# Twelve early loads of an attention and two-MoE kernel issued as 120 and 8 partitions, and one unit's softmax steps in another order

## The chip, the cores and the metric

The kernel runs on 1 core of one Trainium2 chip. The metric is device time in microseconds of one execution. Engines are named as in the profile: PE (TensorE matmul), PEld (its weight loads), DVE (VectorE), ACT (ScalarE), POOL (GpSimd) and SP (SyncE, which here only issues DMAs). A core has 16 DMA engines.

## What is computed

Three stages in a row, each on the output of the one before. Batch 4, 8 heads, 576 positions, head size 64:

```python
scores = scale * np.matmul(q, k.transpose(0, 1, 3, 2))
masks = np.stack([mask_local if h < H // 2 else mask_strided for h in range(H)], axis=0)
attn = softmax(np.where(masks[None], scores, -1e9)); x = attn @ v   # then to (2304, 512)
x = (sigmoid(x @ w_gate) * (x @ w_val)) @ w_out                      # 512 -> 1536 -> 512
x = softplus(x @ w_in) @ w_out2                                      # 512 -> 2048 -> 512
```

The first four heads see a local window of 32 positions, the other four every 32nd position.

## The kernel before, in words

Attention works on 16 units; a unit is one batch and one pair of heads, units 0 and 1 of each batch local, 2 and 3 strided. For a unit, `load` issues its q and K from SP (K of units 0 and 1 from ACT; K of units 2, 3 and 4 as two halves of 64 partitions into `acc` tiles), and `load_v` issues its V. Then, as separate steps: `bias` (a mask product on PE, L1063 or L1075), `scores` (PE, L1095 for units 2 to 4 and L1106 for the others; then DVE's maximum L1124 and subtraction L1125), `exponent` (ACT, L1132), `normalize` (DVE's sum L1139 and reciprocal L1142, POOL's product L1145), `p_transposes` (PE, L1168, then a copy on ACT), `values` (PE, L1188) and `outputs` (ACT L1213, DVE L1216: the high and low halves of x).

The weights come as 64-bit words in pieces of 128 x 512 (`raw`, 512 KB, three buffers, `load_next`, L110). `decode_steps` turns a piece into a high and a low half: first step L132 and L136 on DVE; second step L142 and L149 on DVE, L160 on ACT, L162 and L163 on POOL, and, if it refills, the next `load_next`. A decoding writes two work tiles, f and e; those of the `decp` pool have one buffer each.

The program order of each engine is the order in which the code is written (`manual_schedule`). `first()` is the start of the kernel: units 0 to 4, and the first decodings. `stage(u)` then does one unit each for u from 5 (`START`) on, in four parts with a `yield` after each, and between the parts matmuls of the first MoE (lines L73 to L75, helper `mm3`) are put in. From about 70 us on PE has only MoE matmuls and what little attention is left.

Three more things set when a load starts. `load(..., held=True)`, `load_v(..., held=True)` and `load_next(held=True)` put a one-element memset on POOL (`hold`, L101) that the DMA waits for. The q tiles have three buffers, so q of unit 3 waits until PE is through with the scores of unit 0. And the DMAs take eight completion semaphores in turn: a DMA waits until the one eight before it has landed.

Of the kernel before, what the change touches and what calls it, by code (L numbers as in the profile page):

```python
# [22 lines left out]
P = 128  # L23
# [26 lines left out]
def tile_sparse_attention_moe_moe2(  # L50
# [51 lines left out]

    def load_next(held=False):
        if todo:
            g, m, c = piece = todo.pop(0)
            src = w1[g, m] if g < NG1 else w2[g - NG1, m // 2]
            raw = rawp.tile([P, PIECE], U64, tag="raw", name="raw")
            if held:
                hold(raw.bitcast(F32))
            nc.sync.dma_start(out=raw, in_=src[:, c * PIECE:(c + 1) * PIECE])  # L110
            raws[piece] = raw
            queue.append(piece)
# [764 lines left out]
    def attention():  # L877
        with ExitStack() as actx:
# [48 lines left out]
            def load(i, held=False):  # L927
                b, hp = units[i]
                loc, w, m, ns = dims(i)
                qn, kn = (S, S + STRIDE) if loc else (QPAD, QPAD - HP + SQ)  # L930
                qq = qp.tile([P, QPAD], F32, tag="q", name="qt")
                if held:
                    hold(qq)
                nc.sync.dma_start(out=qq[:, 0:qn], in_=q[b, hp][:, 0:qn])
                if i in paired:
                    kk = paired[i]
                    for h in range(2):
                        rows = slice(h * HP, (h + 1) * HP)
                        nc.sync.dma_start(out=kk[rows, h, 0:kn], in_=k[b, hp][rows, 0:kn])
                else:  # L940
                    kk = kp.tile([P, QPAD], F32, tag="k", name="kt")
                    (nc.scalar if i < 2 else nc.sync).dma_start(
                        out=kk[:, 0:kn], in_=k[b, hp][:, 0:kn]
                    )
                qt[i], kt[i] = qq, kk

            def load_v(i, held=False):
# [8 lines left out]
                n = NL[0] if loc else NS  # L956
                nc.sync.dma_start(out=t[:, 0:n], in_=vl[b, hp] if loc else vs[b, hp - NLP])
                vt[i] = t
# [286 lines left out]
            def first():  # L1245

                decs = [decode_steps(pools, refill) for refill in (False, False, True)]
                swap = lambda: pools.update(f=[other])
# [6 lines left out]
                normalize(0)  # L1255
                load_next(held=True)
                load_v(2)
# [3 lines left out]
                normalize(1)  # L1261
                load_next(held=True)
                load_v(3)
# [8 lines left out]
                normalize(3)  # L1272
                load_next(held=True)
                values(0)
# [17 lines left out]
                pools["scratch"] = None  # L1292
                load_next(held=True)
                load(6)
# [11 lines left out]
                load_next()  # L1306
                next(decs[2])
                yield
                next(decs[2])
                yield  # L1310

            def stage(u):
# [6 lines left out]
                def more():  # L1319
                    if dec:  # L1320
                        next(dec.pop(0))

                if u < NU:
                    bias(u)
                    scores(u)
                if u == START:
                    yield
                if u == START + 2:
# [28 lines left out]
                if u < NU - 2:  # L1357
                    load(u + 2)
                more()
                if u == START + 1:  # L1360
                    exponent(u)
                    nc.scalar.preload_act_table_set("sigmoid_and_others")
                yield
                if u < NU and u != START + 1:
                    exponent(u)
                if len(dec) > 1:
                    more()
                yield
                if u < NU:
                    normalize(u)  # L1370
                values(u - 1)
                outputs(u - 1)
# [211 lines left out]
```

## Times and the profile before

| what | us |
|---|---|
| median of 3 runs | 877.82 |
| the runs | 877.8, 877.82, 880.9 |
| the profiled execution, its own time | 880.17 |
| its span in the trace | 878.0 |

The profiled execution is 2.35 us over the median; 2.17 us of its time lie outside the span. PE is busy 862.9 us of the span; the rows that follow further down are read from this execution. In a row of the timeline the first number is the start in us from the span's start, the second its length, and the bracket at the end is the idle time of the engine just before it, with what ended it.

### The profile page before, as it was taken

What the parts mean: (1) busy time and instruction counts of PE and PEld (TensorE: products, weight loads), DVE (VectorE), ACT (ScalarE), POOL (GpSimd) and SP (SyncE); (2) the same over time, 40 slices, a digit from 0 to 9 for tenths busy, and PEclk for the clock granted to TensorE, in tenths of its full rate; (3) what the DMA queues carried; (4) which work ended last, traced back from release to release, by engine and by line L of the source; (5) the groups of instructions that cost most, each with busy time, mean ns of one, the idle gap of its engine ahead of it and who ended that gap; (6) DMA issues with size and microseconds to landing.
All of it is one profiled execution on the core that took longest, in us unless ns stands there. A gap on an engine that the chain in (4) does not pass through costs nothing.

```text
span 878.0 us, 15217 instructions
## 1 busy us (share of the span) xinstructions
PE 862.9 (98%) x5925; PEld 723.3 (82%) x5925; DVE 600.1 (68%) x897; ACT 422.4 (48%) x684; POOL 490.6 (56%) x394
## 2 busy tenths in 40 slices
PE   7999999999999999999999999999999999999998
PEld 6678788888888888888888888888888888888886
DVE  7887755378888878788865646565757674656574
ACT  4366534233333232333233456666768566655641
POOL 6572511057887788687778525556446963343620
PEclk9899999999999999999999999999999999999999
DMA  9773430044766566557553436655675665545403
GB/s 282 266 249 128 150 130 1 1 144 166 252 230 213 193 241 218 191 196 252 200 185 127 128 101 196 193 195 193 195 259 172 200 213 187 181 141 184 144 1 120
DMA packets 61431, 154.03 MB, mean 175 GB/s; under 512 B 6064, under 2 KB 6576, under 8 KB 61360
## 3 DMA queue, kind: packets, MB, share of 16 engines
q1 hardware_dynamic: 61072, 152.44, 52.1%
q8 instruction: 47, 0.77, 0.4%
q10 hardware_dynamic: 288, 0.62, 0.2%
q14 instruction: 24, 0.20, 0.1%
HBM read 114.76 MB, written 38.27 MB: 174 GB/s over the span
## 4 chain that ended last, share of the span: by engine, by line
PE 72%; DVE 3%; ACT 1%; POOL 1%; issue 1%; DMA 0%; DVEq 0%; POOLq 0%; ACTq 0%; SPq 0%
PE ps_y L73 10%; PE ps_y L74 10%; PE ps_y L75 10%; PE ps_v L74 4%; PE ps_v L75 4%; PE ps_v L73 4%; PE ps_h L74 4%; PE ps_h L75 4%; PE ps_h L73 4%; PE ps_g L74 4%; PE ps_g L75 4%; PE ps_g L73 4%; PE ps_b L73 2%; PE ps_b L74 2%; PE ps_b L75 2%
## 5 line engine op out<-in xcount | busy, mean ns | idle before, releaser
L339 POOL TENSOR_TENSOR b<-b,b 128x512 f32<-128x512 f32 (+1 forms) x42 | 72.4, 1737 | 91.7 <-DVE gl L339 46.2
L313 DVE TENSOR_TENSOR acc<-ps_y,acc 128x512 f32<-128x512 f32 (+1 forms) x100 | 62.1, 633 | 48.0 <-PE ps_y L75 47.6
L252 ACT ACTIVATE gh<-ps_v 128x512 fp32r<-128x512 f32 (+1 forms) x60 | 33.3, 555 | 123.4 <-DVE ps_v L293 123.2
L342 ACT ACTIVATE gh<-b 128x1024 fp32r<-128x1024 f32 (+1 forms) x63 | 57.8, 917 | 40.6 <-DVE b L722 22.7
L478 DVE TENSOR_TENSOR acc<-ps_y,acc 128x512 f32<-128x512 f32 x66 | 44.8, 686 | 39.5 <-PE ps_y L75 38.5
L339 POOL TENSOR_TENSOR gl<-b,gh 128x1024 fp32r<-128x1024 f32 x20 | 49.1, 2456 | 36.5 <-ACT gh L342 36.5
L253 DVE TENSOR_TENSOR gl<-ps_v,gh 128x512 fp32r<-128x512 f32 (+1 forms) x60 | 38.3, 638 | 37.5 <-ACT gh L252 37.5
L199 POOL TENSOR_TENSOR a<-f,e 128x512 f32<-128x512 f32 x32 | 41.4, 1294 | 39.1 <-DVE e L149 39.1
L187 POOL TENSOR_TENSOR pair<-a,pair 128x512 fp32r<-128x512 f32 x32 | 41.5, 1297 | 33.2 <-ACT pair L186 33.2
L339 DVE TENSOR_TENSOR gl<-b,gh 128x1024 fp32r<-128x1024 f32 (+1 forms) x43 | 48.8, 1137 | 14.4 <-ACT gh L342 14.3
L75 PE MATMUL ps_y<-gh,w02l 128*128 128x512 f32 (+1 forms) x144 | 53.7, 373 | 0.4 <-POOL w02l L163 0.4
L73 PE MATMUL ps_y<-gh,w12h 128*128 128x512 f32 (+1 forms) x144 | 54.0, 375 | 0.1
L74 PE MATMUL ps_y<-gl,w12h 128*128 128x512 f32 (+1 forms) x144 | 53.6, 372 | 0.0
L186 ACT ACTIVATE pair<-s 128x512 fp32r<-128x512 f32 x32 | 20.2, 632 | 69.4 <-POOL s L213 54.1
L136 DVE SCALAR_TENSOR_TENSOR f<-raw,ps_x 128x512 uint32<-128x512 uint32 x67 | 46.1, 688 | 9.9 <-POOL w11l L163 2.1
L293 DVE TENSOR_TENSOR ps_v<-ps_v,sg 128x512 f32<-128x512 f32 (+1 forms) x60 | 38.5, 641 | 20.4 <-PE ps_v L75 19.2
L75 PE MATMUL ps_y<-gh,w12l 128*128 128x512 f32 (+1 forms) x140 | 52.2, 373 | 0.2 <-POOL w12l L163 0.2
L73 PE MATMUL ps_y<-gh,w02h 128*128 128x512 f32 (+1 forms) x136 | 51.3, 377 | 0.7 <-ACT acc L311 0.5
L74 PE MATMUL ps_y<-gl,w02h 128*128 128x512 f32 (+1 forms) x136 | 50.7, 372 | 0.2 <-DVE gl L253 0.2
L149 DVE SCALAR_TENSOR_TENSOR e<-raw,ps_x 128x512 f32<-128x512 uint32 x67 | 46.0, 687 | 2.4
L142 DVE TENSOR_SCALAR ps_x<-f 128x512 uint32<-128x512 uint32 x67 | 46.1, 688 | 1.0
L132 DVE TENSOR_SCALAR ps_x<-raw 128x512 uint32<-128x512 uint32 x68 | 46.5, 684 | 0.0
(365 smaller groups left out, 2803.4 us busy)
## 6 DMA issues: line engine op xcount, KB each, us to landing
raw<-in_w_dram SPq DMA_DIRECT2D x68, 512.0 KB, 4.5
in_s<-pair SPq DMA_DIRECT2D x32, 512.0 KB, 3.2
out_s<-pair SPq DMA_DIRECT2D x32, 512.0 KB, 2.9
xh<-in_s SPq DMA_DIRECT2D x64, 256.0 KB, 3.0
xl<-in_s SPq DMA_DIRECT2D x56, 256.0 KB, 3.6
vt<-in_vl_dram SPq DMA_DIRECT2D x8, 640.0 KB, 6.3
out_dram<-acc SPq DMA_DIRECT2D x16, 256.0 KB, 2.2
w10h<-out_s SPq DMA_DIRECT2D x6, 512.0 KB, 4.0
```

Of the source, the lines that this page charges most:

```text
L73: nc.tensor.matmul(ps, lhsT=lh, rhs=rh, start=first, stop=False, **kw)
L74: nc.tensor.matmul(ps, lhsT=lh, rhs=rl, start=False, stop=False, **kw)
L75: nc.tensor.matmul(ps, lhsT=ll, rhs=rh, start=False, stop=last, **kw)
L132: nc.vector.tensor_scalar(out=part, in0=high, scalar1=3, scalar2=0x3FFFFFFF, op0=ALU.logical_shift_left, op1=ALU.bitwise_and,)
L136: nc.vector.scalar_tensor_tensor(out=f, in0=high, scalar=0xC0000000, in1=part, op0=ALU.bitwise_and, op1=ALU.bitwise_or,)
L142: nc.vector.tensor_scalar(out=e, in0=f, scalar1=0xFF800000, scalar2=None, op0=ALU.bitwise_and)
L149: nc.vector.scalar_tensor_tensor(out=e.bitcast(F32), in0=low, scalar=2.0 ** -52, in1=x.bitcast(F32), op0=ALU.mult, op1=ALU.mult,)
L187: nc.gpsimd.tensor_tensor(out=l, in0=src, in1=h.bitcast(F32), op=ALU.subtract)
L313: nc.vector.tensor_tensor(out=y, in0=ps[:, 0:n], in1=y, op=ALU.add)
L339: eng.tensor_tensor(out=out, in0=a, in1=b, op=ALU.subtract)
L342: nc.scalar.activation(out=op[0], in_=src, func=AF.Copy)
L478: nc.vector.tensor_tensor(out=y, in0=ps, in1=y, op=ALU.add)
```

## The change

- `copy_rows` issues a load either as one DMA or as two, of partitions 0 to 119 and 120 to 127. Two are issued for q of units 2, 3 and 4, for V of units 0 to 4, and for the four pieces that `first()` loads with `load_next(held=True)`: twelve loads.
- In `load(3)` the two halves of K are issued ahead of q.
- The third decoding leaves `first()` and is done in `stage(5)`, both its steps in one go, after the scores and the exponent of unit 5. That exponent moves ahead of it, to just after the scores. The decoding that `stage(5)` had of its own starts after `normalize(5)`.

```diff
+    few = 15 * (P // 16)
+
+    def copy_rows(out, src, apart):
+        for rows in (slice(0, few), slice(few, P)) if apart else (slice(0, P),):
+            nc.sync.dma_start(out=out[rows], in_=src[rows])
+
-    def load_next(held=False):
+    def load_next(held=False, apart=False):
...
-            nc.sync.dma_start(out=raw, in_=src[:, c * PIECE:(c + 1) * PIECE])
+            copy_rows(raw, src[:, c * PIECE:(c + 1) * PIECE], apart)
...
-                nc.sync.dma_start(out=qq[:, 0:qn], in_=q[b, hp][:, 0:qn])
+
+                def load_q():
+                    copy_rows(qq[:, 0:qn], q[b, hp][:, 0:qn], NLP <= i <= NPAIR)
+
+                if i != NPAIR - 1:
+                    load_q()
                 if i in paired:
...
+                    if i == NPAIR - 1:
+                        load_q()
...
-                nc.sync.dma_start(out=t[:, 0:n], in_=vl[b, hp] if loc else vs[b, hp - NLP])
+                copy_rows(t[:, 0:n], vl[b, hp] if loc else vs[b, hp - NLP], i <= NPAIR)
...
-                decs = [decode_steps(pools, refill) for refill in (False, False, True)]
+                decs = early_decs
+                decs += [decode_steps(pools, refill) for refill in (False, False, True)]
...
-                load_next(held=True)
+                load_next(held=True, apart=True)
...
                 load_next()
-                next(decs[2])
                 yield
-                next(decs[2])
                 yield
+
+            early_decs = []
...
                 if u == START:
+                    exponent(u)
                     yield
...
-                more()
+                if u > START:
+                    more()
+                else:
+                    next(early_decs[2])
+                    next(early_decs[2])
...
-                if u < NU and u != START + 1:
+                if u < NU and u > START + 1:
                     exponent(u)
-                if len(dec) > 1:
+                if u > START and len(dec) > 1:
                     more()
                 yield
                 if u < NU:
                     normalize(u)
+                if u == START:
+                    more()
```

The line `load_next(held=True)` changes so in four places. What the change moves on the engines stands in the built order. On SP, from the third q load on, before (`qt` is q, `vt` V, `acc2` and `acc0` the homes of K of units 2 and 3; DMAHW0 to 7 are the eight completion semaphores):

```order
L934 DMA qt_148<-in_q_dram 128x622
L939 DMA acc2_65<-in_k_dram 64x612 x2
L934 DMA qt_152<-in_q_dram 128x622 [waits DMAHW1_49,PE_49]
L939 DMA acc0_63<-in_k_dram 64x612 [waits DMAHW0_49]
L939 DMA acc0_63<-in_k_dram 64x612
L957 DMA vt_156<-in_vl_dram 128x1280 [waits DMAHW2_49]
L957 DMA vt_158<-in_vl_dram 128x1280 [waits DMAHW3_49]
L110 DMA raw_331<-in_w1_dram 128x512 [waits DMAHW4_49,Pool_49]
```

and in the changed kernel:

```order
L107 DMA qt_148<-in_q_dram 120x622
L107 DMA qt_148<-in_q_dram 8x622
L950 DMA acc2_65<-in_k_dram 64x612 x2
L950 DMA acc0_63<-in_k_dram 64x612 [waits DMAHW0_49]
L950 DMA acc0_63<-in_k_dram 64x612 [waits DMAHW1_49]
L107 DMA qt_153<-in_q_dram 120x622 [waits DMAHW2_49,PE_49]
L107 DMA qt_153<-in_q_dram 8x622 [waits DMAHW3_49]
L107 DMA vt_158<-in_vl_dram 120x1280 [waits DMAHW4_49]
L107 DMA vt_158<-in_vl_dram 8x1280 [waits DMAHW5_49]
L107 DMA vt_161<-in_vl_dram 120x1280 [waits DMAHW6_49]
L107 DMA vt_161<-in_vl_dram 8x1280 [waits DMAHW7_49]
L107 DMA raw_335<-in_w1_dram 120x512 [waits DMAHW0_49,Pool_49]
```

K of unit 3 no longer stands behind q of unit 3 and its wait for PE, and each split load takes two of the eight semaphores.

On DVE at units 4 and 5 (`sl0` is the softmax tile of unit 4, `sl1` that of unit 5; `raw_411` the third piece, `raw_579` the fourth), before:

```order
L1142 RECIPROCAL st_642<-st_642 128x2x5
L132 TENSOR_SCALAR ps_x_658<-raw_411 128x512
L136 SCALAR_TENSOR_TENSOR f_656<-raw_411,ps_x_658 128x512
L142 TENSOR_SCALAR ps_x_667<-f_656 128x512
L149 SCALAR_TENSOR_TENSOR e_657<-raw_411,ps_x_667 128x512
L1124 TENSOR_REDUCE st_720<-ps_s_677 128x5x2
L1125 TENSOR_TENSOR sl1_110<-ps_s_677,st_720 128x5x2x64
L132 TENSOR_SCALAR ps_x_746<-raw_579 128x512
L136 SCALAR_TENSOR_TENSOR f_744<-raw_579,ps_x_746 128x512
L1139 TENSOR_REDUCE st_720<-sl1_110 128x2x5
```

and in the changed kernel, where the third piece is `raw_420` and the fourth `raw_590`:

```order
L1155 RECIPROCAL st_654<-st_654 128x2x5
L1137 TENSOR_REDUCE st_719<-ps_s_676 128x5x2
L1138 TENSOR_TENSOR sl1_110<-ps_s_676,st_719 128x5x2x64
L138 TENSOR_SCALAR ps_x_746<-raw_420 128x512
L142 SCALAR_TENSOR_TENSOR f_744<-raw_420,ps_x_746 128x512
L148 TENSOR_SCALAR ps_x_750<-f_744 128x512
L155 SCALAR_TENSOR_TENSOR e_745<-raw_420,ps_x_750 128x512
L1152 TENSOR_REDUCE st_719<-sl1_110 128x2x5
L1154 TENSOR_SCALAR st_719<-st_719 128x2x5
L1155 RECIPROCAL st_719<-st_719 128x2x5
L138 TENSOR_SCALAR ps_x_767<-raw_590 128x512
```

The maximum and subtraction of unit 5 now stand ahead of the third decoding, and its sum and reciprocal ahead of the fourth. On ACT the exponent of unit 5 (`sl1`) stood behind a decoding step and a copy, before:

```order
L1132 ACTIVATE sl0_109<-sl0_109 128x640
L160 ACTIVATE w01h_68<-f_656 128x512
L1174 ACTIVATE pt_729<-ps_p_730 128x2x320
L1132 ACTIVATE sl1_110<-sl1_110 128x640
L1213 ACTIVATE xh_61<-ps_o_758 128x320
```

and in the changed kernel it stands ahead of both, and the decoding step has gone behind the copy:

```order
L1145 ACTIVATE sl0_109<-sl0_109 128x640
L1145 ACTIVATE sl1_110<-sl1_110 128x640
L1187 ACTIVATE pt_729<-ps_p_730 128x2x320
L166 ACTIVATE w01h_68<-f_744 128x512
L1226 ACTIVATE xh_61<-ps_o_770 128x320
```

The order of PE's and of POOL's instructions is the same in both kernels.

## Rows read from the trace of the kernel before

**Rows 1.** The page, part 1: busy time, share, instructions.
```profile
PE 862.9 (98%) x5925; PEld 723.3 (82%) x5925; DVE 600.1 (68%) x897; ACT 422.4 (48%) x684; POOL 490.6 (56%) x394
```

**Rows 2.** Waits of PE, 0 to 70 us: total us, times, longest.
```profile
PE ps_s L1095 <- DMA acc<-in_k_dram: 2.3, 2, 1.7
...
PE ps_o L1188 <- issue: 1.1, 2, 1.0
```

**Rows 3.** Timeline, 5.9 to 18 us: SP, DVE, POOL and PE, units 2 and 3.
```profile
5.98 0.33 SPq L934 DMA_DIRECT2D qt<-in_q_dram  x1
...
6.36 1.10 SPq L939 DMA_DIRECT2D acc<-in_k_dram  x2
...
12.69 1.33 PE L1095 MATMUL ps_s<-acc,qt 128*64 128x108 f32 x24 [1.68 <-DMA acc<-in_k_dram]
...
13.02 0.21 DVE L1142 RECIPROCAL st<-st 128x10 f32<-128x10 f32 x1
...
14.07 0.83 DVE L1124 TENSOR_REDUCE st<-ps_s 128x12 f32<-128x648 f32 x1 [0.83 <-PE ps_s L1095]
...
16.92 1.42 POOL L1145 TENSOR_TENSOR ss<-ss,st 128x324 f32<-128x324 f32 x2 [2.11 <-DVE st L1142]
...
17.93 1.02 PE L1168 MATMUL ps_p<-one,ss 128*128 128x128 f32 x6 [0.42 <-ACT acc L1172]
```

**Rows 4.** DMA issues, 6.3 to 6.8 us: count, KB each, us to landing.
```profile
qt<-in_q_dram SPq DMA_DIRECT2D x1, 311.0 KB, 4.1
acc<-in_k_dram SPq DMA_DIRECT2D x1, 153.0 KB, 5.6
```

**Rows 5.** DMA queue of the instructions, 8 to 20 us: packets, MB, share.
```profile
q8 instruction: 2, 0.03, 1.2%
```

**Rows 6.** Stretches: length, busy us by engine, PEclk, DMA share, GB/s.
```profile
8.80:10.00 1.20, 1.05 (x23) 1.09 (x24) 1.20 (x2) 0.65 (x1) 0.00 (x0) 1.00 1.03 230
12.40:14.00 1.60, 1.31 (x25) 1.20 (x25) 0.77 (x3) 0.43 (x1) 0.62 (x1) 1.00 0.98 353
```

**Rows 7.** Timeline, values of unit 1 on PE, 18.9 to 21.4 us.
```profile
18.88 0.55 PE L1188 MATMUL ps_o<-acc,vt 64*64 64x32 f32 x24
...
20.38 1.00 PE L1188 MATMUL ps_o<-acc,vt 64*64 64x32 f32 x48 [0.95 <-issue]
```

**Rows 8.** Timeline, 32 to 42 us: unit 5 on DVE, POOL and PE.
```profile
32.73 0.67 DVE L132 TENSOR_SCALAR ps_x<-raw 128x512 uint32<-128x512 uint32 x1
...
35.56 0.82 DVE L1124 TENSOR_REDUCE st<-ps_s 128x10 f32<-128x640 f32 x1
...
38.97 0.81 DVE L1139 TENSOR_REDUCE st<-sl 128x10 f32<-128x640 f32 x1
...
40.38 1.40 POOL L1145 TENSOR_TENSOR sl<-sl,st 128x320 f32<-128x320 f32 x2 [2.67 <-DVE st L1142]
...
41.16 0.44 PE L1168 MATMUL ps_p<-one,sl 128*128 128x128 f32 x2 [1.11 <-POOL sl L1145]
```

**Rows 9.** Timeline, 44 to 55 us: units 6 and 7.
```profile
44.43 0.69 DVE L136 SCALAR_TENSOR_TENSOR f<-raw,ps_x 128x512 uint32<-128x512 uint32 x1 [0.67 <-POOL w01l L163]
...
53.59 1.42 POOL L1145 TENSOR_TENSOR ss<-ss,st 128x324 f32<-128x324 f32 x2 [3.28 <-DVE st L1142]
...
54.40 1.21 PE L1168 MATMUL ps_p<-one,ss 128*128 128x128 f32 x6
```

**Rows 10.** Waits of SP, whole span: total us, times, longest.
```profile
SPq L934 <- DMA qt<-in_q_dram: 1.2, 1, 1.2
```

**Rows 11.** Timeline: SP's K of unit 4, and its scores on PE.
```profile
18.82 1.24 SPq L939 DMA_DIRECT2D acc<-in_k_dram  x2
...
26.59 2.35 PE L1095 MATMUL ps_s<-acc,qt 128*32 128x128 f32 x36
28.87 0.58 PE L73 MATMUL ps_g<-xh,w00h 128*128 128x512 f32 x1
```

**Rows 12.** One stretch, columns as in rows 6.
```profile
22.25:29.07 6.82, 6.66 (x138) 5.10 (x139) 4.84 (x9) 2.60 (x5) 3.58 (x5) 0.50 0.77 272
```

More of the change, by code (lines that the diff above doesn't have):

```diff
@@ L1261, in first @@
                 normalize(1)
-                load_next(held=True)
+                load_next(held=True, apart=True)
                 load_v(3)
@@ L1272, in first @@
                 normalize(3)
-                load_next(held=True)
+                load_next(held=True, apart=True)
                 values(0)
@@ L1292, in first @@
                 pools["scratch"] = None
-                load_next(held=True)
+                load_next(held=True, apart=True)
                 load(6)
```

## The prediction

> **What bounds the kernel now.** I read the page first: PE is busy for 862.9 of 878.0 us [rows 1]. So 15.1 us of the span are not PE work, and no edit here takes PE work away; only idle time of PE can be won, and whatever delays PE in the first 60 us is paid in full, since the matmuls behind it form one queue. Second, the waits of PE over the first 70 us [rows 2]: the scores of units 2 and 3 wait 2.3 us for K (the longest wait 1.7), and the values wait 1.1 us for nothing that the profile shows ("issue"). Third, the timeline at each of these places, which tells who is free when the wait ends: unit 3's scores [rows 3], the values of unit 1 [rows 7], the normalization of unit 5 [rows 8]. These are the places that the change touches.
>
> **Part 1: loads of unit 3.** PE begins unit 3's scores at 12.69 after 1.68 us of idle, so it could have begun at 11.01 [rows 3]. q of unit 3 was issued at 5.98 and landed 4.1 us later, at about 10.1; K's first half was issued at 6.36 and took 5.6, to about 12.0 [rows 3, 4]. The two halves are 2 x 153 KB, 0.313 MB; in the stretch in which they move, the core takes 230 GB/s [rows 6], so 1.36 us after q they should be down, at 11.5. PE begins 1.2 us after that. A landing is the last of 16 engines' shares, and an instruction packet of 16 KB (0.03 MB for two) goes through one DMA engine beside the loads twice between 8 and 20 us [rows 5]. My reading, an inference that no row proves, is that one engine runs behind because it carries the instructions too, and the last share of each load is its share.
>
> The change does two things here. K of unit 3 no longer waits behind q, which is held until PE has left unit 0's scores; it goes as soon as a semaphore is free. And 120 = 15 x 8 rows can be dealt as 8 rows to each of 15 engines, the 8 rows left as one each to 8 of them, so that one engine has nothing of the split loads. If that is the one behind, unit 3's loads are down by about 11 and the scores start at about 11.1. What is late next is DVE: it is busy until 13.02 + 0.21 = 13.23 and takes unit 3's maximum at 14.07 [rows 3]. So only 14.07 - 13.23 = 0.84 goes on, through DVE's sums to POOL's product of unit 2 at 16.92 and PE's transposes at 17.93 [rows 3]. Bounds: 0 (the loads land as late as now) and 0.84 (DVE). I take 0.8.
>
> The Trainium skill (DMA: Bandwidth & Descriptors, section "Why a DMA increments its semaphore by 16 and not by 1") says that a DMA issued from SP runs on the largest number of engines up to 16 that divides its slowest dimension, the lowest-numbered first: 15 engines for 120 rows, 8 for 8. The trace of before has only transfers of 128 and 64 rows and cannot show it. By that rule the engine left out is the last, and nothing in the rows says whether it is the one behind.
>
> **Part 2: the stall of unit 1's values.** PE does 24 of the 72 instructions of unit 1's values at 18.88, then stands 0.95 us for "issue" and goes on at 20.38 [rows 7]. The first 24 have just used the same V tile and the same transposes, so no operand is missing; I take this as PE waiting for its own instructions, whose packet shares an engine with the early loads. If that engine is relieved, the stall shrinks. Bounds 0 and 0.95; the row has no other candidate, and four V loads and three pieces of words leave that engine alone before 20 us, so I take 0.9. Cover behind it: scores of unit 4 begin at 26.59, and their K was issued from 18.82 on [rows 11]; the second half from about 19.5; at the 5.6 us of rows 4 it lands at about 25.1. With PE 1.7 us earlier the scores want it at 24.9, and SP's issue is 0.8 earlier with POOL's release, so it lands at 24.3 and just covers.
>
> **Part 3: unit 5.** PE waits 1.11 us at 41.16 for POOL's product of unit 5, which waited for DVE until 40.38 [rows 8]. DVE did the third decoding first, four instructions from 32.73 on (0.67 each, to 35.5), then the maximum at 35.56, and the sum only at 38.97, behind the next decoding [rows 8]. After: maximum and subtraction take the place from 32.8 to 34.5, ACT's exponent fits in while DVE does the four decoding steps (34.6 to 37.4), the sum begins at 37.4 and the reciprocal ends at 38.7, 1.6 us earlier. But POOL's two products of the third decoding are now late, since their inputs come 2 us later: at 1.3 us each they end at about 39.4, and only then the product of unit 5 starts, against 40.38: 1.0 earlier. At PE that is worth 0.9, as the copy of unit 4's transposes on ACT now stands behind unit 5's exponent and is some 0.2 later. Not all of this lasts. The next decoding on DVE waits for POOL's low half of the one before (0.67 at 44.43), and at 54.40 PE's transposes of unit 7 take 1.21 us, where six of them took 1.02 at 17.93 (which also had to wait halfway): they run right behind POOL's product, from 53.59 on, which had waited for DVE [rows 3, 9]. DVE does the same work before it; by my count it is only 0.3 us earlier at 46 us. So of 0.9 about 0.3 is left behind unit 7. Bounds 0 and 0.9; I take 0.3.
>
> **Part 4: what the split costs.** Twelve more issues at 0.33 us or a little more (the row of 5.98 [rows 3]) are some 4 us of SP, which mostly stands waiting for POOL or PE. On the path is one: the second issue of q of unit 2 stands ahead of unit 2's K, 0.33 us. That K is behind q and K of units 0 and 1 in the DMA engines anyway, so I take 0.1, bounds 0 and 0.4. Each split load also takes two of eight completion semaphores, so SP waits for loads that are nearer: V of unit 0 for q of unit 2, V of unit 1 for K of unit 2. Queued behind them are the other V loads and the words. Such a wait shows once now, 1.2 us [rows 10]. V of unit 1 goes out about 0.8 later than now and is wanted only at 18.88 less 0.8, so I cost this at nothing; if V of unit 0 were held up as long as 1.2 us it would cost up to 0.8, what part 1 wins.
>
> **The sum.** -0.8 - 0.9 - 0.3 + 0.1 = -1.9 us. The profiled execution took 880.17, 2.17 more than its span, so one like it would take 878.3; the median of the runs is 877.82, and there the sum gives 875.9. This is the forecast: 0.2% faster.
>
> **The rivals.** First, **the split relieves nothing**: the engine behind is one of the fifteen, or it is no single engine, and both parts of a load land when the one did. Unit 3's last share then still comes at about 12.4, the stall stays, and part 3 alone is left with part 4: -0.3 + 0.1, and 877.6. For it: no row names the engine. Against it: unit 3's K is issued earlier in any case. The Trainium skill (the same page, section "Rules for kernel authors") speaks for this rival: it advises against two transfers to disjoint partitions in place of one, as they only serialize on the same engines. By that rule the time is this rival's.
>
> Second, **slower: narrow transfers move at the rate of K's halves**. With the DMA engines busy throughout, the core takes 230 GB/s in the stretch of the 64-row halves and 353 in that of V and words [rows 6]. If 120 rows go like 64, everything from q of unit 3 to q of unit 4 comes later: V 640 + 640 + 384 + 384, words 512 + 512, q 288 KB, together 3.44 MB, 15.0 us at 230 in place of 9.7 at 353. After unit 3's K (11.5) and q (1.35) that is 27.9, and K of unit 4 at 1.36 lands at 29.2. Scores of unit 4, now at 26.59 [rows 11], would begin 2.6 late, while parts 1 and 2 are gone; with part 3, +2.3: 880.1. The point from which it decides is a rate under 272 GB/s (3.75 MB in the 13.8 us from 12.8 to 26.6). For it: the halves' rate. Against: a row set of 120 covers nearly all partitions, where a half covers 64.
>
> Third, **the clock**: from 22.25 to 29.07 us the granted clock was 0.50 of full, 1.2 GHz, and 1.00 in the other stretches shown [rows 6]; PE had stood for 0.95 us in that neighbourhood [rows 7, 12]. PE is busy 6.66 us in it. The matrix instructions there are short ones, held by issue as much as by the clock, so full clock would give not half of that but, I estimate, about 2 us. If a start with less idle time keeps the clock up, it adds 2 us: 873.9. The fast runs may have no such dip already (the profiled execution is 2.35 over the median), so I give this little.
>
> **How the numbers follow.** Forecast 0.50 (with its own bounds, 0 to 2.7 of gain and 1.2 of cost: 874.7 to 877.0 in most cases), the split relieves nothing 0.22, slower by narrow transfers 0.15, clock 0.13. The range 872.6 to 880.2 takes in the forecast, the first rival and the clock, and most of the second up to its price. A measurement of this kernel tells about 0.5%, 4.4 us, from no change: faster than 873.4 takes the clock and all the rest, 0.11; slower than 882.2 takes narrow transfers and a held V together, 0.05; within 0.5% the rest, 0.84.
>
> **What would show it.** Part 1: unit 3's scores start near 11.1 with little idle time, and DVE's maximum follows at 13.2 with no wait; wrong if the idle time before them stays over 1 us. Part 2: the values of unit 1 run as 72 instructions with no "issue" gap. Both together: the first L73 matmul, now at 28.87 [rows 11], begins at about 27.2. Part 3: the wait of 1.1 us for POOL at unit 5 goes to 0.2 or less, and the gain from unit 5 on shrinks to 0.3 by unit 7. The second rival shows as GB/s near 230 between 12 and 20 us and a wait for DMA at unit 4's scores; the third as a granted clock of 1.00 between 20 and 29 us. What would make the sum wrong altogether is a wait of SP for a semaphore that holds a word load past the time that DVE wants it.

## The result, and the profile after

The changed kernel took 884.72 us (median of six runs, 884.26 to 885.41), the kernel before 878.41 beside it; the ratio is 1.0067, with a 95% interval of 1.0050 to 1.0083. It is slower by some 6.3 us, where 1.9 less was predicted. The profiled run of the changed kernel took 884.26, its span is 882.4 us against 878.0 [rows 1]: 4.4 of the 6.3 us can be followed in the two traces. Most of the rest is the profiled run of before, which at 880.17 lay 1.8 over the median of its kernel, while that of the changed kernel lay 0.5 under.

PE does the same 5,925 matrix instructions, and is busy for 864.3 us, 1.4 more than in [rows 1]. This is the page, part 1: busy time, share, instructions.

```profile
span 882.4 us, 15234 instructions
...
PE 864.3 (98%) x5925; PEld 724.5 (82%) x5925; DVE 600.9 (68%) x897; ACT 422.7 (48%) x684; POOL 490.7 (56%) x394
```

So 3.0 of the 4.4 us are idle time, and 1.4 are the same instructions taking longer. The loss arises in the first 31 us. The timeline of PE, after, at the places where it stood (start, length, instructions, and in brackets the idle time before and what ended it):

```profile
11.92 0.83 PE L1108 MATMUL ps_s<-acc,qt 128*64 128x108 f32 x13 [0.57 <-DMA qt<-in_q_dram]
13.58 0.77 PE L1108 MATMUL ps_s<-acc,qt 128*64 128x108 f32 x11 [0.82 <-issue]
...
16.30 1.35 PE L1201 MATMUL ps_o<-pt,vt 64*64 64x32 f32 x72 [1.14 <-DMA vt<-in_vl_dram]
...
23.20 1.00 PE L1201 MATMUL ps_o<-acc,vt 64*64 64x32 f32 x48 [2.99 <-issue]
...
28.86 0.90 PE L1201 MATMUL ps_o<-acc 54*64 54x54 f32 x24 [1.33 <-issue]
...
31.05 2.35 PE L1108 MATMUL ps_s<-acc,qt 128*32 128x128 f32 x36
```

These are unit 3's scores, unit 0's values, unit 1's values, unit 3's values and unit 4's scores. Unit 3's scores begin at 11.92 instead of 12.69 [rows 3], earlier as planned, though not at the 11.1 forecast. Then unit 3's scores are cut in two by a new wait of 0.82 for "issue", PE waits 1.14 for V of unit 0, and the "issue" wait in unit 1's values is 2.99 where it was 0.95 [rows 7]. Unit 4's scores follow at 31.05, against 26.59 [rows 11], and **they wait for nothing**: the 4.46 us are lost ahead of them. Up to these scores PE has done the same 500 matrix instructions in both kernels, before in 21.08 us of busy time, after in 21.92 (columns as in [rows 6]: length, busy us by engine, granted clock, DMA share, GB/s):

```profile
0.00:26.59 26.59, 21.08 (x500) 16.95 (x500) 20.16 (x41) 12.97 (x25) 15.20 (x39) 0.92 0.89 282
```

```profile
0.00:31.05 31.05, 21.92 (x500) 17.57 (x500) 20.85 (x41) 12.91 (x25) 16.36 (x40) 0.90 0.93 226
```

So 3.62 of the 4.46 us are idle time and 0.84 are longer busy time, with the granted clock lower on the mean (0.90 against 0.92). Behind that the distance shrinks at unit 5 and grows back by unit 7: 3.52 at unit 5's transposes (41.16 before [rows 8]), 4.54 at unit 7's (54.40 before [rows 9]), and 4.4 at the end of the span.

```profile
44.68 0.44 PE L1181 MATMUL ps_p<-one,sl 128*128 128x128 f32 x2
...
58.94 1.24 PE L1181 MATMUL ps_p<-one,ss 128*128 128x128 f32 x6 [0.41 <-POOL ss L1158]
```

The stretches say what is behind the idle time. After, from 12 to 20 and from 20 to 30 us (columns as above):

```profile
12.00:20.00 8.00, 5.62 (x138) 4.62 (x138) 6.13 (x12) 4.13 (x10) 4.87 (x10) 1.00 0.96 213
20.00:30.00 10.00, 5.68 (x167) 4.91 (x159) 6.92 (x11) 3.92 (x9) 3.53 (x6) 0.73 0.99 224
```

The same two of the kernel before:

```profile
12.00:20.00 8.00, 6.09 (x138) 4.92 (x138) 6.93 (x15) 4.79 (x11) 4.40 (x11) 1.00 0.95 323
20.00:30.00 10.00, 9.46 (x196) 7.53 (x197) 6.96 (x12) 3.81 (x8) 5.14 (x6) 0.66 0.76 246
```

The DMA engines are as busy from 12 to 20 us, 0.96 against 0.95, and move 213 GB/s instead of 323. From 20 to 30 they are still full (0.99) where before they had begun to run dry (0.76): they work off what they are behind. And PE's instructions come by these engines: between 8 and 20 us one packet of them went through after, where two did before [rows 5].

```profile
q8 instruction: 1, 0.02, 0.6%
```

SP now waits for the landing of earlier loads, over the first 40 us 4.2 us behind V and 2.2 behind words (total us, times, longest); before, its one such wait was 1.2 [rows 10]. The DMA engines stay full meanwhile, at 0.96 and 0.99, so these waits follow full engines and leave none empty.

```profile
SPq L107 <- DMA vt<-in_vl_dram: 4.2, 2, 2.1
SPq L107 <- DMA raw<-in_w_dram: 2.2, 2, 1.4
```

### The profile page after: what moved, and what is told of

It reads as the page before. It is cut to its first block, busy times and chain, and to the rows that moved or that the text cites. A ratio compares the mean times of both kernels' runs of the same rounds, so it can differ in the third digit from the quotient of the medians.

```text
span 882.4 us, 15234 instructions
## 1 busy us (share of the span) xinstructions
PE 864.3 (98%) x5925; PEld 724.5 (82%) x5925; DVE 600.9 (68%) x897; ACT 422.7 (48%) x684; POOL 490.7 (56%) x394
## 4 chain that ended last, share of the span: by engine, by line
PE 68%; DVE 4%; ACT 3%; POOL 3%; issue 1%; DMA 0%; DVEq 0%; POOLq 0%; ACTq 0%; SPq 0%
PE ps_y L73 9%; PE ps_y L74 9%; PE ps_y L75 9%; PE ps_v L73 4%; PE ps_v L74 4%; PE ps_v L75 4%; PE ps_g L73 4%; PE ps_g L74 4%; PE ps_g L75 4%; PE ps_h L74 3%; PE ps_h L75 3%; PE ps_h L73 3%; PE ps_b L73 2%; PE ps_b L74 2%; PE ps_b L75 2%
```

## The experiments

The theory after the result, **rate**: a transfer of less than all 128 rows moves at some 200 to 245 GB/s; the loads fall behind, and with them V and PE's instructions. Its rivals: **two transfers** (twice the issues and semaphores cost it, wherever the cut falls) and **order** (one of the other two parts of the change costs it). All ratios are to the kernel before, with 95% intervals; the profile columns are those of one run each, in us but for the rate. The last column is the same work in each kernel, 500 matrix instructions, so more busy time in it goes with a lower granted clock.

| Kernel | Ratio | GB/s, 12 to 20 us | PE idle for "issue", 6 to 32 us | first MoE matmul | PE busy up to unit 4's scores |
|---|---|---|---|---|---|
| before | 1 | 323 | 1.1 | 28.87 | 21.1 |
| changed | 1.0067 (1.0050 to 1.0083) | 213 | 5.1 | 33.33 | 21.9 |
| all loads whole | 0.9990 (0.9974 to 1.0006) | 282 | 2.8 | 30.09 | 21.1 |
| only the splits | 1.0058 (1.0035 to 1.0081) | 216 | 1.9 | 33.14 | 23.8 |
| cut at 112 | 1.0021 (1.0007 to 1.0036) | 268 | 2.7 | 30.31 | 21.2 |
| five V split | 1.0070 (1.0048 to 1.0093) | 226 | 3.1 | 32.75 | 22.4 |
| V of units 0, 1 split | 1.0035 (1.0015 to 1.0056) | 273 | 2.9 | 31.91 | 23.6 |
| V of units 2 to 4 split | 1.0022 (1.0010 to 1.0034) | 269 | 4.2 | 31.40 | 21.7 |
| words split | 1.0027 (1.0010 to 1.0044) | 255 | 4.1 | 32.46 | 21.4 |
| whole, 1.9 MB more | 1.0028 (1.0014 to 1.0043) | 316 | under 0.2 | 30.92 | 21.8 |

**All loads whole.** The changed kernel, with the third argument of every `copy_rows` False.

```
-                    copy_rows(qq[:, 0:qn], q[b, hp][:, 0:qn], NLP <= i <= NPAIR)
+                    copy_rows(qq[:, 0:qn], q[b, hp][:, 0:qn], False)
```

> The changed kernel with the twelve loads whole again; K of unit 3 ahead of its q, and unit 5's early exponent with the moved decodings, stay. Theory 'rate' (a transfer of 120 rows moves at some 200 to 245 GB/s, as the stretches of the changed kernel's trace show, against 353 before; the loads fall behind and the fetch of PE's instructions and V of unit 0 with them): the loss goes entirely, 876 to 879 us, ratio to before 0.998 to 1.001; stretch 12 to 20 us back at 240 to 360 GB/s, PE's 'issue' idle time ahead of unit 1's values back under 1.5 us. Rival 'two transfers' (twice the issues and semaphores cost it, wherever the cut falls): the same here. Rival 'order' (K ahead of q, or the moved exponent and decoding, costs it): 883 to 885 us, ratio about 1.006.

0.9990 (0.9974 to 1.0006), 879.22 us beside 879.13. The loss is gone entirely, so "order" is out. The "issue" wait went to 0.68 in unit 1's values, but the one in unit 3's values is 2.16, against 0.16 before; that comes back below.

**Only the splits.** The kernel before with `copy_rows` and the twelve splits, its own order kept.

> The kernel before with the twelve splits of 120 and 8 rows and nothing else. Theories 'rate' and 'two transfers': the whole loss and the gains of the other two parts missing, 884 to 887 us (ratio 1.006 to 1.010), GB/s of 200 to 245 from 12 to 20 us. Rival 'order': 877 to 879 us, ratio 1.000.

1.0058: the loss is there without the other two parts. Here PE waits 2.01 us ahead of unit 3's scores and 1.26 for V of unit 3; the places differ from the changed kernel's, the sum does not. Nor is it idle time in the main. Unit 4's scores begin at 30.86, 4.27 late, and 2.69 of that are longer busy time (23.77 against 21.08): the granted clock is 0.66 on the mean from 12 to 20 us, where it was 1.00 before and in the changed kernel.

```profile
0.00:30.86 30.86, 23.77 (x500) 19.15 (x500) 20.77 (x41) 13.12 (x25) 17.03 (x41) 0.85 0.93 227
```

```profile
12.00:20.00 8.00, 6.51 (x107) 5.83 (x108) 5.58 (x11) 3.07 (x7) 4.61 (x11) 0.66 0.95 216
```

**Cut at 112.** As many transfers and issues, other rows.

```
-    few = 15 * (P // 16)
+    few = 14 * (P // 16)
```

> The changed kernel with the cut at row 112 in place of 120: as many transfers, issues and semaphores, but both numbers of rows are multiples of 16. Theory 'rate' in its narrow form (it is the 120 rows that are slow): back at 300 GB/s or more in the stretches at full DMA share, 876 to 880 us. Rival 'two transfers': as the changed kernel, 883 to 886 us and SP's waits for earlier transfers (4.2 us for V, 2.2 for words) still there. Rival 'order': 883 to 886 us too, with the rate back.

Between the two: 1.0021, and 268 GB/s from 12 to 20 us. "Two transfers" wanted 883 to 886 us and got 880.92. The narrow form of "rate" (multiples of 16 are fast) was wrong as well: the rate did not come back to 300. What holds of these four kernels is that the time goes with the rate in the kernel.

**Loads alone**, to measure the disputed rate by itself.

```
+    stretch((0, 128))
+    stretch((0, 120))
+    stretch((0, 112))
+    stretch((0, 64))
+    stretch((120, 128))
+    stretch((0, 120), (120, 128))
+    stretch((0, 112), (112, 128))
+    stretch((0, 64), (64, 128))
+    stretch((0, 128))
```

> Leaves out the whole computation: nine stretches of eight loads of words (4 KB a row) one behind another, each stretch after the last has landed: 128 rows; 120; 112; 64; the last 8; 120 and 8; 112 and 16; 64 and 64; 128 again; then zeros to the output. Theory 'rate': 128 rows at 330 to 370 GB/s, 120 rows at 200 to 245, 120 and 8 at 245 or less, 64 rows near 230, 112 rows and 112 and 16 near the 128 rows. Rival 'two transfers': 120 alone within 10% of 128, and both pairs of unequal parts, 112 and 16 as well, clearly slower than their single transfers.

Windows inside the stretches of 128 rows, 120, 112, 64, 120 and 8, 112 and 16, 64 and 64, and 128 again (length, busy VectorE and GpSimd, granted clock, DMA share, GB/s):

```profile
12.00:18.00 6.00, 0.90 (x10) 0.00 (x0) 1.00 1.03 413
22.00:38.00 16.00, 1.33 (x13) 0.00 (x0) 1.00 1.01 226
42.00:52.00 10.00, 1.28 (x12) 0.00 (x0) 1.00 1.01 239
55.00:63.00 8.00, 1.34 (x13) 0.00 (x0) 1.00 0.77 154
69.00:85.00 16.00, 1.34 (x13) 0.00 (x0) 1.00 0.99 246
88.00:102.00 14.00, 1.28 (x12) 0.00 (x0) 1.00 1.04 234
105.00:119.00 14.00, 1.33 (x13) 0.00 (x0) 1.00 1.04 241
121.20:130.00 8.80, 1.49 (x14) 0.00 (x0) 1.00 1.04 419
```

A buffer is loaded anew as soon as its own last load has been taken over, so a window holds some bytes of the stretch behind it. When VectorE takes over the loads tells the same without the windows:

```profile
12.88 0.15 DVE L67 COPY sink<-t 128x1 uint32<-128x1 uint32 x1 [0.84 <-DMA t<-in_w_dram]
...
17.99 0.15 DVE L67 COPY sink<-t 128x1 uint32<-128x1 uint32 x1 [1.00 <-DMA t<-in_w_dram]
...
21.77 0.15 DVE L67 COPY sink<-t 128x1 uint32<-128x1 uint32 x1 [1.99 <-DMA t<-in_w_dram]
...
39.05 0.15 DVE L67 COPY sink<-t 128x1 uint32<-128x1 uint32 x1 [2.43 <-DMA t<-in_w_dram]
```

From the first to the second of these rows are four loads of 128 rows, one every 1.28 us; from the third to the fourth seven of 120 rows, one every 2.47.

Whole transfers move 413 and 419 GB/s; everything else that keeps the engines full moves 226 to 246, 120 rows by themselves as well. This settles it against "two transfers": the single transfer of 120 rows is as slow as the pair. It also corrects the expectation at 112 rows, which go at 239 and not near the full rate. One thing it leaves open: by themselves 112 and 16 rows (234) are no faster than 120 and 8 (246), yet the kernel cut at 112 moves 268 where the changed one moves 213, and loses a third as much. No run here tells why.

**Which loads, and how much each.** Four kernels split some of the loads only; the edits are the conditions of `apart`, as above.

> The changed kernel with only the five loads of V in two parts; q and the words go whole. Theory 'backlog' (what costs is the DMA time lost to the slow parts: 2.76 MB at 225 instead of 353 GB/s is an estimate of 4.5 of the 9.4 us that all twelve lose): V of unit 0 late again at PE (some 1 us), PE's 'issue' idle time in units 1 and 2 between 1.5 and 4 us, time between the whole loads' 879 and the changed kernel's 885: 880 to 883 us. Rival 'words alone' (only the 512 KB transfers are long enough to hold up PE's instructions): 879 us.

> The changed kernel with only the four pieces of words in two parts; q and V go whole. Theory 'backlog': 2.1 MB, an estimate of 3.4 of the 9.4 us: V of unit 0 no longer late, 879.5 to 882 us. Rival 'words alone': 883 to 885 us.

> The changed kernel with only V of units 0 and 1 in two parts (1.3 MB). Theory 'it is the early V' (V of unit 0 late at PE, and the PE instructions wanted at 18 to 20 us behind both): nearly all that e5_v_split lost, 883 to 886 us. Theory 'backlog by bytes': about half of it, 880.5 to 883 us.

> The changed kernel with only V of units 2 to 4 in two parts (1.4 MB). Theory 'it is the early V': little left, 878.5 to 881 us. Theory 'backlog by bytes': about half of what e5_v_split lost, 880.5 to 883 us, through V of unit 2 late at PE (1.3 us there) and the instructions of units 1 and 2.

Words 1.0027 and five V 1.0070; of the V, 1.0035 by units 0 and 1 and 1.0022 by units 2 to 4. So "words alone" and "the early V alone" are out: every group costs, and the two halves of V (1.3 and 1.4 MB) together cost 0.57%, about the 0.70% of all five. (With V of units 0 and 1 alone the 883.50 us lie in the range that "the early V" gave; but the kernel before took 880.06 beside it, and the ratio is half of that of all five. All these kernels contain the other two parts of the change; against whole loads at 0.9990 each ratio is 0.10% more. The three q were not split alone.) The expectation for the five V (880 to 883 us) was too low, 885.95: per byte the V cost more than the words, and words and V together more than the changed kernel loses; what is behind at 13 to 30 us isn't paid by the byte. (The expectations call the second "issue" wait one of unit 2; it stands in unit 3's values, and the V in the place of an accumulator is unit 3's.)

**More bytes, none cut**: does it need the cut at all, or only engines that are behind? All loads whole, and further whole loads that nobody reads.

```
+    def more_bytes():
+        for _ in range(2):
+            t = next(spare)
+            nc.sync.dma_start(out=t, in_=w2[0, 0][:, 0:t.shape[1]])
```

> The changed kernel with all twelve loads whole (e1_unsplit), and ten further whole loads of 196 to 205 KB into places that nobody reads, two behind each of V of units 1, 4 and the first words among them: 2.0 MB, an estimate of 5.7 us of DMA time at 353 GB/s, some 60% of what the splits lose. Theory 'backlog' (late loads and late PE instructions, however the engines come to be behind): 881 to 884 us, PE's 'issue' idle time in units 1 and 2 at 3 us or more together, V of unit 0 late, though no load is split. Rival 'the split as such' (parts, their semaphores and issues): 878 to 880 us, as e1_unsplit.

The first try told nothing: 1.0111, but ScalarE's copy of unit 1's transposes waited 10.6 us for a spare load, since the place it went to is where that copy writes.

> As e6_more_bytes, whose further loads went in part to a place where a tile of unit 1 lies, so that ScalarE's copy waited 10.6 us for one of them; here they go to places of which nobody makes use in this stretch: ten whole loads of 147 to 205 KB, 1.9 MB, an estimate of 5.3 us of DMA time at 353 GB/s. Theory 'backlog' (late loads and late PE instructions, however the engines come to be behind): 881 to 884 us, and 'issue' idle time of PE in units 1 and 2 of 3 us or more together, though no load is cut. Rival 'the cut as such': 878 to 880 us, as with whole loads and no more bytes.

1.0028, 882.69 us, in the expected range, but by another road than expected: no "issue" wait worth the name, one of 4.43 us ahead of unit 3's values. Timeline, SP and PE:

```profile
16.78 2.43 SPq L107 DMA_DIRECT2D acc<-in_w_dram  x2
...
19.26 0.43 SPq L116 DMA_DIRECT2D acc<-in_vs_dram  x1
...
26.14 1.54 PE L1211 MATMUL ps_o<-acc 54*64 54x54 f32 x48 [4.43 <-DVE acc L164]
```

The releaser named is a decoding on VectorE that these matmuls don't read; what they read and what was issued late is V of unit 3, at 19.26, behind spare loads that themselves held SP for 2.43 us. From its issue to its landing it took 6.7 us, so it was there at about 25.96, and PE began at 26.14:

```profile
acc<-in_vs_dram SPq DMA_DIRECT2D x1, 384.0 KB, 6.7
```

So engines that are behind cost time without any cut, but part of this one is SP's own wait, which the splits do not have in that form.

**Instructions beside loads.** Is the "issue" time really PE waiting for its instructions behind the loads? A kernel with nothing but small matmuls and loads.

> Leaves out the whole computation: PE alone with 600 matmuls of 64x32 four times over (no loads beside it; whole loads of 128 rows; 120 and 8 rows; 64 and 64), then 400 matmuls of 128x108 the same way; sixteen loads of 512 KB at most beside each stretch. Theory 'instructions come by the same DMA engines': PE's stretches have more idle time put down to issue beside loads than without, by 0.5 to 3 us for each 16 KB of instructions, and the longest beside the cut loads; the instruction packets take longer there (1.3 against 1.0 us). Rival 'the idle time has another cause': the four stretches of one kind take the same time within 0.3 us.

This first form showed nothing: its matrix instructions waited for one another (128.21 us for 1200, 107 ns each), PE was never short of instructions, and the stretches of the first kind were alike within 0.01 us; in the second kind the longest, 76.56 against 74.21 us, was the one meant to have no loads beside it.

```
+            r, h = m // 2 % 2 * 64, m % 2 * 64
+            nc.tensor.matmul(
+                ps[h:h + 64, m // 2 % 2, 0:n], lhsT=lhs[r:r + 64, 0:64],
+                rhs=rhs[r:r + 64, 0:n], start=True, stop=True,
```

> Leaves out the whole computation: as e8_fetch, whose matmuls took 107 to 214 ns one after another and left PE no stretch short of instructions; here 1200 matmuls of 64x32 a stretch go round the four quarters of the array as those of the values do, at some 23 to 30 ns each, five stretches: no loads beside it; whole loads; 120 and 8 rows; 64 and 64; no loads. Theory 'instructions come by the same DMA engines': with no loads little idle time put down to issue, beside loads 0.5 to 3 us for each 16 KB of instructions, the most beside the cut loads, so that those stretches are 5 us or more longer. Rival 'the idle time has another cause': all five within 1 us.

SP ran ahead of PE, so the loads lay beside the first 75 us of PE's work, and again from 125 to 145 us, and not beside the stretches meant; the windows are cut by what the DMA did. Whole loads, 120 and 8 rows, no loads (length, busy PE, weight loads, VectorE, GpSimd, clock, DMA share, GB/s):

```profile
21.00:41.00 20.00, 13.27 (x479) 12.87 (x476) 0.92 (x16) 0.00 (x0) 1.00 0.94 364
42.00:62.00 20.00, 10.88 (x384) 10.49 (x384) 0.74 (x11) 0.00 (x0) 1.00 0.97 249
...
150.00:170.00 20.00, 19.91 (x740) 19.78 (x740) 0.00 (x0) 0.00 (x0) 1.00 0.02 5
```

And PE's timeline in them:

```profile
35.77 3.63 PE L79 MATMUL ps<-rhs,lhs 64*64 64x32 f32 x128 [2.83 <-issue]
41.97 3.64 PE L79 MATMUL ps<-rhs,lhs 64*64 64x32 f32 x128 [2.56 <-issue]
50.08 3.64 PE L79 MATMUL ps<-rhs,lhs 64*64 64x32 f32 x128 [4.48 <-issue]
57.10 3.64 PE L79 MATMUL ps<-rhs,lhs 64*64 64x32 f32 x128 [3.38 <-issue]
...
143.35 31.82 PE L79 MATMUL ps<-rhs,lhs 64*64 64x32 f32 x1152 [4.76 <-issue]
175.53 23.79 PE L79 MATMUL ps<-rhs,lhs 64*64 64x32 f32 x865 [0.37 <-issue]
```

The same instructions: with idle DMA engines PE stops for 0.37 us now and then; beside full engines it stops after every 128 matrix instructions (256 with their weight loads), for 2.3 to 2.8 us beside whole loads and 2.3 to 4.8 beside cut ones. In 20 us it gets 740 matrix instructions done with no loads, 479 beside whole ones and 384 beside 120 and 8 rows. So "issue" here is PE waiting for instructions that queue behind data, and the cut loads make it longer.

**The other two parts, one at a time**, since all loads whole was level with before where two gains were expected.

```
+                if i != NPAIR - 1:
+                    load_q()
...
+                    if i == NPAIR - 1:
+                        load_q()
```

> The kernel before with K of unit 3 ahead of its q, and nothing else. Theory 'given back' (the start of unit 3's scores is earlier, and a wait for instructions or for V between 18 and 27 us takes it back): unit 3's scores at 11.9 to 12.1 us, PE's wait ahead of them 1.0 us instead of 1.68, time within 0.15% of the kernel before (877.5 to 880.5 us on a chip where that takes 879). Rival 'the gain stays': 0.8 us less, ratio 0.999. Rival 'this part costs': ratio 1.001 to 1.002.

1.0000 (0.9985 to 1.0016). Unit 3's scores at 11.99, unit 0's values at 14.32 instead of 15.03, 0.71 gained; then 0.41 of waiting for V of unit 3 and 1.61 of "issue" in its values, and unit 4's scores at 27.30, 0.71 late. Its timeline:

```profile
11.99 1.33 PE L1102 MATMUL ps_s<-acc,qt 128*64 128x108 f32 x24 [0.98 <-DMA qt<-in_q_dram]
...
14.32 1.68 PE L1195 MATMUL ps_o<-pt,vt 64*64 64x32 f32 x72 [0.20 <-ACT pt L1179]
...
25.12 0.90 PE L1195 MATMUL ps_o<-acc 54*64 54x54 f32 x24 [1.61 <-issue]
```

> The kernel before with unit 5's exponent right behind its scores and the third decoding moved to it, all loads whole and q of unit 3 ahead of its K. PE's wait for the normalizing of unit 5 (1.11 us) at 0.3 us or less, and some 0.5 us of it back in each of units 6 and 7 (as the changed kernel's trace has it): ratio 0.999 to 1.000. Rival 'this part costs': ratio 1.001 to 1.002, with a wait that is not in the kernel before, between 30 and 70 us.

1.0004 (0.9990 to 1.0018). The wait at unit 5 is gone; two come in its place, at the values of unit 6 and at the transposes of unit 7:

```profile
41.00 0.44 PE L1178 MATMUL ps_p<-one,sl 128*128 128x128 f32 x2
...
51.09 0.92 PE L1198 MATMUL ps_o<-pt,vt 54*64 54x54 f32 x48 [0.36 <-ACT pt L1184]
...
55.26 1.24 PE L1178 MATMUL ps_p<-one,ss 128*128 128x128 f32 x6 [0.39 <-POOL ss L1155]
```

PE is 0.99 us behind the kernel before at unit 4's scores (27.58 against 26.59; 2.71 us of "issue" in unit 3's values), 0.16 ahead at unit 5's transposes (41.00 against 41.16) and 0.86 behind at unit 7's (55.26 against 54.40 [rows 9]): 1.15 gained, 1.02 given back.

**A version that might beat both**: all loads whole, and V of unit 3 ahead of the second piece of words.

> The changed kernel with all loads whole and V of unit 3 issued ahead of the second piece of words instead of behind it. Theory 'given back': PE's wait for V of unit 3 (0.42 us with whole loads, 2.45 where only the words are cut) goes, the words land some 1 us later and are not waited for: 0.3 to 0.6 us less than with whole loads, ratio to the kernel before 0.998 to 0.9995. Rival 'the words are then late': ScalarE's and GpSimd's decoding of the second piece waits for it and PE's first MoE matmul comes later: ratio 1.000 to 1.002.

1.0014 (1.0002 to 1.0026). Its profiled run is 1.7 us shorter in span than the kernel before, and the first MoE matmul is at 27.30, so the words were not late. Its twelve runs are slower nevertheless, 880.52 at the median, and the profiled one, 878.54, is the fastest of them: one profile of this kernel doesn't settle 2 us. No version here beats the kernel before.

## Why the prediction was wrong

**The step that failed is part 4, what the split costs.** It counted issues and semaphores, 0.1 us with bounds of 0 and 0.4, and took the transfers' speed as unchanged. The trace of before had the row that spoke against it, 230 GB/s for transfers of 64 rows [rows 6], and the second rival used it. Loads alone show 226 to 246 GB/s for everything cut against 413; in the kernel 213 against 323. By the runs the term is some 5 to 7 us, not 0.1: 1.0058 of 878 with the splits alone is 5.1, 1.0067 less 0.9990 is 6.8. The sign that the prediction named for a sum wrong altogether, words that come past the time that VectorE wants them, was there as well: VectorE waited 1.84 us for the first piece. Not a wait of SP did that, for the piece was issued at 12.71, 0.57 later than before; it took longer to land. PE did not wait for what was decoded from it.

```profile
21.09 0.69 DVE L138 TENSOR_SCALAR ps_x<-raw 128x512 uint32<-128x512 uint32 x1 [1.84 <-DMA raw<-in_w_dram]
```

**The second rival had the mechanism and a third of the price** (2.3 us, chance 0.15). It priced only K of unit 4, whose scores it let wait for DMA. They did not wait; PE was later than K. The price was due earlier, at V of unit 0 (1.14) and at PE's instructions (0.82, 2.99 and 1.33, against 0.95 and 0.16). Its argument against itself, that 120 rows cover nearly all partitions, was worth nothing: 120 rows alone go at 226. The sign it named, GB/s near 230 between 12 and 20 us, was there, at 213. That the 230 of [rows 6] is the rate of the halves was itself a reading; loads alone bear it out, 64 and 64 rows at 241.

**Part 2 had the sign wrong.** The "issue" wait is a wait for instructions; the loads alone with matmuls bear that out. But the change doesn't relieve the engine that carries them. It keeps all engines full for longer, and the wait grew from 0.95 to 2.99. That one engine is behind and that it is the one left out stayed an inference; with the splits the landing was late altogether, and no run tells which engine carried the packet. That one was left out agrees with loads alone: they have 1,456 packets under 512 B, which is the sum of one for each engine of each DMA, 15 engines for 120 rows, 8 for 8, and 16 for all other shapes. (Part 2 also counts three pieces of words before 20 us; in both traces SP issues two by then.)

**Part 1 was right where it was looked at**: 0.77 earlier at the scores, 0.71 at unit 0's values with K first alone, within the bound of 0.84 that VectorE sets. It was to begin at 11.1; q, now behind K, holds it to 11.9. What was missing is the next bound. The prediction named VectorE as late next and stopped there; PE then came sooner to the same instruction packets and waited longer, 1.61 instead of 0.16, so nothing is left by unit 4's scores.

**Part 3 was right in kind**: the 1.1 us wait went, 1.15 gained where 0.9 was worked out. Of the 0.3 that was to be left behind unit 7 some 0.1 is there by itself, since unit 6's values now wait for ScalarE as well (0.36), which the prediction had not seen; in the changed kernel 0.94 was won by unit 5's transposes (4.46 to 3.52) and all of it given back by unit 7's (4.54).

**The first rival** (the split relieves nothing, 877.6) is the rule of the Trainium skill, DMA: Bandwidth & Descriptors, section "Rules for kernel authors", that two transfers to disjoint partition halves serialize. The measurement goes beyond it: in sequence at the old rate they would cost nothing, and halves run at 0.58 of it (241 against 413), 120 and 8 rows at 0.6 (246).

**The clock** moved the other way than the third rival had it. From 22 to 36 us (columns as above), after and then before, the mean granted clock is 0.63 against 0.76. With the two levels 0.5 and 1 that is some 10 of the 14 us at 1.2 GHz against 7, and it follows a stretch in which PE stood idle more. The third line is the low stretch itself, 10.31 us at 0.50, where it was 6.82 before [rows 12]:

```profile
22.00:36.00 14.00, 11.47 (x215) 8.92 (x223) 8.46 (x14) 4.78 (x9) 5.15 (x6) 0.63 1.00 226
```

```profile
22.00:36.00 14.00, 13.21 (x246) 9.51 (x244) 10.70 (x18) 4.92 (x9) 6.19 (x9) 0.76 0.65 227
```

```profile
24.55:34.86 10.31, 8.98 (x146) 6.79 (x145) 6.29 (x10) 3.11 (x7) 3.99 (x6) 0.50 1.01 226
```

So the clock is part of what the splits cost, and no term of the prediction has it on that side. In the two traces the 1.4 us of longer busy time go with it. Over the runs it may be more: of the 23 runs of before beside "all loads whole" the four at a mean clock of 0.993 or 0.994 took 881.03 to 882.20 us, and the changed kernel's four at the same clock 884.26 to 884.85. At the like clock the difference is some 3 us, so by this estimate about half of the 6.3 us goes with the lower clock. The rival's doubt was right: five of those 23 are at a mean of 1.000, with hardly a dip.

## What to carry to other kernels

A load that is cut by rows to spare one engine is paid by all of them: measure the rate of the cut transfer alone before counting its issues. (That rate told that the cut costs, not how much: 112 and 16 rows were no faster alone, and cost a third.) At the start of a kernel, where the DMA engines are full, count the instruction packets among the loads. Idle time of PE that no operand explains can be the wait for instructions queued behind data, and an earlier start was given back here at the next such wait. When a row of the trace prices a rival, follow the delay to every consumer of the loads, the first one above all.

## What the runs showed of the hardware that was not expected

- Only transfers of all 128 rows go at 413 to 419 GB/s; 120, 112, and pairs of 120 and 8, 112 and 16, 64 and 64 go at 226 to 246, with the DMA engines' share at 0.99 to 1.04 in all of them. Why whole transfers are so much faster is open: no run here tells it.
- PE's instructions come through the same DMA engines: 256 of them cost PE up to 0.39 us with the engines idle, and 2.3 to 4.8 with the engines full. The Trainium skill (Runtime: NRT & Kernel Launch, section "Instruction fetch mechanics") has this cost as mostly hidden; for matrix instructions of 28 ns (3.63 us for 128) beside loads the measurement differs.
- The granted clock goes with much of the spread of the kernel before: of the 23 beside "all loads whole", the five at a mean of 1.000 took 877.28 to 877.74 us, the seven at 0.996 or less 880.29 to 882.20. The eleven in between spread from 878.03 to 881.92, so the mean clock is not all of it. The changed kernel's six runs are all at 0.991 to 0.994.
